# Five instruction lists made anew: block 2 and its statistics first, transposed copies ahead of evictions

## The chip, the core and the metric

The kernel runs on one core of a Trainium2 chip. The core has a matrix engine (PE, with its weight loads shown as PEld), a vector engine (DVE), an activation engine (ACT), a general engine (POOL) and a queue engine (SP) that issues most of the DMAs. The engines run side by side and wait for one another through semaphores. The metric is the device time of one execution in microseconds (us), lower is better. Before the change it is 225.8 us, the median of 3 runs from 225.59 to 225.95.

## The reference

One block of 2048 tokens of width 512 goes through a layer norm, then through two branches whose results are added to the input. All matrices are bfloat16.

```python
xn = layernorm(x)                                   # (2048, 512)
# A: 32 heads of width 16, each token sees 8 tokens back, 2 apart
q, k, v = split(xn @ wqkv)
logits[s, w] = q[s] . k[s - 2 w] / 4                # w = 0..7, masked before the start
A = (softmax(logits) weighted sum of v[s - 2 w]) @ wo
# B: gated unit with mixing over tokens
z  = gelu(xn @ w_in)                                # (2048, 1792)
z1 = z[:, :896];  z2 = layernorm(z[:, 896:])
g  = w_sp @ z2 + b_sp                               # (2048 x 2048) @ (2048 x 896)
B  = (z1 * g) @ w_out
out = x + A + B
```

## The kernel before

The tokens are cut into 16 blocks of 128 rows; x block b is loaded by the task `ldx<b>`. Each piece of work is a named task, made by a call of `T` (a compute task) or `dma` with the engine it runs on, the keys of what it reads and writes, and the function that emits its instructions. `Plan.add` derives from the keys which task has to wait for which. At the end of `build_kernel` five lists of task names (`plan.orders`: PE, ACT, DVE, POOL, SP) give the order on each engine; `Plan.schedule` follows them, and `Plan.emit` writes each engine's program in that order, with a semaphore wait wherever a task depends on another engine. An engine works strictly in its list's order: if the next task has to wait, all behind it wait too. A task of ACT's list whose name starts with `ld` or `st` issues a DMA from ACT's own queue and holds ACT's list in the same way.

The stages, in order, with the lines of the matrix work:

- Norm and transposition of blocks 0 to 3. `bnst<b>` (L665) and `bnag<b>` (L668) on DVE give mean and variance, `rstd<b>` (L670) on POOL the inverse deviation by a power, `norm<b>` (L680) on DVE the normed block. PE transposes it in two halves, `xTr<b>a` and `xTr<b>b` (L696), by a product with an identity made on POOL (`ident1`, `nident1`), and ACT copies each half out of PSUM (`xTe<b>a`, `xTe<b>b`, L703). Block 0 is transposed only centred (`ctr0`, `ctr1`, L673 and L675) for its first use; `xNr` and `xNe` (L717, L721) transpose the normed block 0 for all later uses. `warm`, `fill0` and `fill1` (L637) are products of ones that nothing reads.
- Blocks 0 to 3 times the second half of `w_in`, 448 columns at a time: `z2_<b>_<h>a` and `z2_<b>_<h>b` (L906, two products each), then `z2g<b>_<h>` on ACT (L913, gelu). The four quarters of this weight are `ldw_in2a_0`, `ldw_in2b_0` from SP and `ldw_in2a_1`, `ldw_in2b_1` from ACT; a and b are the first and second 448 columns, 0 and 1 the upper and lower rows.
- Blocks 4 to 15 are normed in the same way and transposed by a DMA from SP, `xTd<b>` (L684). For four groups of 512 tokens, `Q<j>_<c>` and `K<j>_<c>` (L749, four products each) give one quarter of the heads' queries and keys; `QKe<j>_<c>` on ACT (L757) copies the pair out, and small `halo` copies (L763) carry the last keys into the next group's buffer. `ldq` and `ldk` load the weights. `z2_4` to `z2_15` (L883) and `z2g4` to `z2g15` (L889) go on with the gated branch, `z2s<b>` (L938) sums squares on ACT.
- On DVE `prod<j>_<c>` (L772) and `padd<j>_<n>` (L780) form the logits' products; PE sums them in `lg0_0` and `lg2_0` (L807).
- `z1_<b>` (L926) and `z1g<b>` (ACT, L932) are the first half of the gate, `V<b>` (L733) and `Ve<b>` (ACT, L737) the values. `zn<b>` norms z2, partly on ACT, partly on DVE.
- The mixing over tokens in eight pairs of blocks, `P1_<t>` to `P7_<t>` (L1044), by a scheme with seven products in place of eight that needs sums made on DVE (`S13`, `S2`, `S4`, `T1` to `T4`), and the softmax (`sm`, `ssub`, `sexp`, `sz`, `srec`, `sattn`), the weighted values (`pv`, `pva`, `pvc`) and the gating (`g11` to `g22`, `u<b>`) beside it. `out<b>_0` (L1251 and L1255, eleven products) makes an output block; `fin<b>_0` copies it out and `st` stores it.

PSUM has eight banks of 512 columns, dealt out in the order in which tasks are added, so the bank of each task is the same whatever the lists say. A product may write a bank only when the copy of the bank's former content is done.

The places that matter at the start are these. x block b lies in slot b modulo 8, so `ldx8` can be issued only when all readers of block 0 (the last is `norm0`) are done. `ldx4` to `ldx7`, `ldq` and `ldk` carry a made-up read of `w_in2b_1`, which holds them on SP until that quarter has landed:

```python
for b in range(4, min(8, NB)):
    ld_x(b, "sp", after=[("w_in2b", 1)])
```

Of the kernel before, what the change touches and what calls it, by code (L numbers as in the profile page):

```python
# [14 lines left out]
class Plan:  # L15
# [313 lines left out]
def build_kernel(nc, A_x, A_wqkv, A_wo, B_x, B_w_in, B_w_sp, B_b_sp, B_w_out, out, report=False, sched_kw=None,  # L329
# [90 lines left out]
    with ExitStack() as es:  # L420
# [10 lines left out]
        def A(name, n, o2_=0):  # L431
            return ar[:, off[name] + o2_: off[name] + o2_ + n]
# [4 lines left out]
        def Fv(name, n, o2_=0):  # L437
            return fp[:, foff[name] + o2_: foff[name] + o2_ + n]
# [832 lines left out]
        for t in range(NT):  # L1271
# [11 lines left out]
            if t >= 1:  # L1283
# [3 lines left out]

        plan.orders = [
            """
                warm xTr0b fill0 xTr0a fill1 z2_0_0b z2_0_1b z2_0_0a xTr1a xTr1b z2_0_1a xNr z2_1_0a z2_1_0b z2_1_1a  # L1290
                xTr2a xTr2b z2_1_1b z2_2_0a z2_2_0b xTr3a z2_2_1a xTr3b z2_2_1b z2_3_0a z2_3_1a z2_3_1b z2_3_0b K0_3
                K0_0 K0_1 Q0_0 K0_2 Q0_1 Q0_2 Q0_3 Q1_0 K1_0 Q1_1 K1_1 K1_2 Q1_2 Q1_3 K1_3 z2_4 z2_5 z2_6 z2_7 K2_0
                Q2_0 K2_1 Q2_2 Q2_1 K2_2 Q2_3 K2_3 z2_8 z2_9 z2_10 z2_11 Q3_0 K3_0 K3_1 Q3_1 K3_2 Q3_2 K3_3 z2_12 Q3_3
                z2_13 lg0_0 z2_14 z1_14 z2_15 z1_15 z1_12 z1_13 z1_10 z1_11 z1_9 z1_8 z1_6 z1_4 z1_5 z1_7 z1_3 z1_0
                z1_2 V12 V13 V14 z1_1 lg2_0 V15 V8 V11 V10 V6 V7 V9 V4 V5 V1 V2 V0 V3 P1_0 P5_0 P6_0 P2_0 P7_0 P3_0
                P1_1 bits P4_0 P2_1 P6_1 P5_1 P7_1 P3_1 P1_2 P4_1 P5_2 P2_2 P6_2 out15_0 P7_2 P3_2 P1_3 P4_2 out14_0
                P6_3 P5_3 P2_3 P3_3 P7_3 P1_4 P5_4 out12_0 P6_4 P4_3 P2_4 out13_0 P7_4 P3_4 P1_5 P4_4 out10_0 P6_5
                P2_5 P5_5 P7_5 P3_5 out11_0 P4_5 P1_6 P5_6 out8_0 P2_6 P6_6 out9_0 P7_6 P3_6 P5_7 out6_0 P1_7 P4_6
# [5 lines left out]
                QKe1_1 halo0_2 QKe1_2 QKe1_3 z2s3 z2g4 halo0_1 z2g5 halo0_3 halo0_0 z2s4 halo1_1 halo1_0 z2g6 halo1_2
                z2g7 z2s5 QKe2_0 z2s6 QKe2_1 QKe2_2 z2s7 QKe2_3 z2g8 z2s8 z2g9 z2g10 z2s9 z2g11 z2s10 QKe3_0 z2s11
                halo2_1 QKe3_1 halo1_3 zn3 QKe3_2 zn0 z2g12 QKe3_3 halo2_2 z2g13 z2s12 lge0 z2g14 z2s13 z1g14 biasf
                z2g15 zn6 halo2_0 halo2_3 z1g15 z1g12 zn8 z1g13 z1g10 zn1 z1g11 z2s14 z1g9 z2s15 z1g8 z1g6 zn2 z1g4
                zn11 z1g5 z1g7 lge1 zn9 z1g0 z1g3 z1g2 Ve12 Ve13 zn10 zn4 Ve14 z1g1 lge2 lge3 zn5 Ve15 Ve10 zn7 Ve11
                Ve7 Ve8 Ve6 Ve4 Ve5 Ve9 ldxr0 sexp3 Ve2 cA_0 Ve3 Ve1 Ve0 cE_0 cB_0 g11_0 sexp2 cA_1 g21_0 os14_0 g11_1
                cB_1 cE_1 sexp1 os15_0 cA_2 g11_2 cB_2 ldxr1 cE_2 g21_1 ldxr2 g21_2 cA_3 cB_3 sexp0 g11_3 cE_3 os12_0  # L1310
                fin14_0 cA_4 cE_4 fin15_0 st0_0_0 cB_4 os13_0 g21_3 fin12_0 os11_0 fin13_0 g11_4 st1_0_0 ldxr3 os10_0
                ldxr4 cA_5 cB_5 cE_5 fin10_0 g21_4 g11_5 os9_0 g21_5 os8_0 cA_6 fin8_0 cB_6 fin11_0 os6_0 fin9_0
# [8 lines left out]
                bnst12 bnag14 bnag12 prod0_2 bnst15 padd0_1 norm14 bnag15 norm13 prod0_3 zv0 zq1 norm12 padd0_2 norm15
                prod1_0 zv1 prod1_2 zb0 zq2 padd1_0 zv2 padd1_1 zb1 prod2_0 zb2 prod2_2 padd2_0 zq3 prod3_2 padd2_1
                prod3_0 zv3 padd3_0 padd3_1 T3_0 zb3 T3_2 S13_0 zn13 S2_0 T1_0 zn14 zn12 smask T2_0 S4_0 zn15 T4_0
                T3_3 T3_1 T1_3 T1_1 sm1_3 sm2_3 T2_1 sm3_3 ssub3 T1_2 T2_3 T2_2 T4_3 T4_2 sz1_3 T4_1 sz2_3 sz3_3 sm1_2
                srec3 sm2_2 sattn3 sm3_2 pv14 ssub2 pv15 g22_0 sz1_2 g12_0 S13_1 sz2_2 S2_1 pva2048_0 sz3_2 sm1_1 u15
# [70 lines left out]
```

## Time and profile before

| what | value |
|---|---|
| median of 3 runs | 225.8 us (225.59 to 225.95) |
| profiled execution, whole time | 225.37 us |
| profiled execution, span from first to last instruction | 223.6 us |
| granted PE clock (mean) | 1.000 |
| PE busy | 219.7 us (98%) |
| DVE busy | 207.3 us (93%) |
| ACT busy | 134.2 us (60%) |
| POOL busy | 89.6 us (40%) |

By stage (the view that sums each engine's busy time over stretches of the span):

| stretch of the span | what runs on PE | PE | DVE | ACT |
|---|---|---|---|---|
| 0 to 5.22 us | warm-up, first transposition | 5.22 | 2.50 | 2.44 |
| 5.22 to 12.55 | blocks 0 to 3 | 7.28 | 5.34 | 5.54 |
| 12.55 to 55.40 | Q, K and z2 | 42.69 | 42.54 | 39.45 |
| 55.40 to 98.40 | logits, z1, V | 42.90 | 42.86 | 42.25 |
| 98.40 to 205.60 | mixing and outputs | 106.83 | 107.00 | 37.78 |
| 205.60 to 223.60 | the end | 15.69 | 7.08 | 6.75 |

Matmuls are pipelined and their ends are modelled, so a PE that is shown busy can hold short waits: the starts of its instructions have to be compared with the pace at which equal instructions follow each other elsewhere. In a chain of waits, a row gives start, length, engine, line and number of instructions of a piece. A row of the timeline gives start, length of one or of a merged run, engine, line, operation, shapes, and in brackets the idle time before it and what ended that.

### The profile page before, as it was taken

Reading aid. Unit: us, or ns where it says so; the run is one execution under the profiler, and the core shown is the slowest. Engines: PE = TensorE matmul, PEld = TensorE weight load, DVE = VectorE, ACT = ScalarE, POOL = GpSimd, SP = SyncE. Lnnn points to the kernel's source line nnn. Section 1 sums busy time; section 2 is a strip of 40 time slices with the busy share of each in tenths; the row PEclk is TensorE's granted clock in tenths of the full one; section 3 lists DMA queues with packets and bytes.
Section 4 is the critical chain, followed back from the end, with each engine's and each line's share of the span. In section 5 each row is a group of like instructions: output and inputs, shape, how many; then the busy total and the mean of one; then the engine's idle time right before and its main releaser. Section 6 shows DMA issues by size and latency. Waiting matters only on the chain.

```text
span 223.6 us, 3124 instructions
## 1 busy us (share of the span) xinstructions
PE 219.7 (98%) x1166; PEld 122.4 (55%) x1180; DVE 207.3 (93%) x236; ACT 134.2 (60%) x241; POOL 89.6 (40%) x38
## 2 busy tenths in 40 slices
PE   8999999999999999999999999999999999999995
PEld 7555555554677776655555454544545544444544
DVE  4699999999999999999999999999999999999810
ACT  4769899999999999977333304324304216224442
POOL 4355559965000090000000899945999900000000
DMA  6884442790000002879689997949589696428352
GB/s 222 275 185 117 97 117 51 197 201 0 3 0 0 0 0 85 176 199 215 154 166 174 233 130 157 186 118 200 173 165 228 140 193 154 99 51 179 118 104 94
DMA packets 77716, 29.96 MB, mean 134 GB/s; under 512 B 68731, under 2 KB 75401, under 8 KB 77702
## 3 DMA queue, kind: packets, MB, share of 16 engines
q1 hardware_dynamic: 74566, 25.08, 53.2%
q10 hardware_dynamic: 3136, 4.69, 6.4%
q8 instruction: 9, 0.15, 0.3%
q14 instruction: 5, 0.04, 0.1%
HBM read 9.05 MB, written 2.10 MB: 50 GB/s over the span
## 4 chain that ended last, share of the span: by engine, by line
PE 98%; issue 0%; ACT 0%
PE ps L1044 38%; PE ps L749 12%; PE ps L926 11%; PE ps L1255 11%; PE ps L883 8%; PE ps L733 6%; PE ps L1251 6%; PE ps L906 3%; PE ps L637 2%; PE ps L807 1%; PE ps L696 0%; ACT arena L703 0%; ACT arena L1264 0%; PE ps L717 0%; PE ps L1237 0%
## 5 line engine op out<-in xcount | busy, mean ns | idle before, releaser
L1044 PE MATMUL ps<-arena 128*128 128x448 f16 (+1 forms) x448 | 86.7, 352 | 0.0
L866 POOL TENSOR_TENSOR arena<-arena,fpool 128x128 bf16<-128x128 f32 x2 | 49.9, 24946 | 45.6 <-DVE arena L862 45.6
L1044 PEld LDWEIGHTS ps<-arena 128*128 128x128 f16 (+1 forms) x448 | 43.8, 98 | 41.4
L1189 DVE TENSOR_TENSOR arena<-arena 128x4096 bf16<-128x4096 bf16 x16 | 36.2, 2282 | 0.0
L772 DVE TENSOR_TENSOR arena<-arena 128x8192 bf16<-128x8192 bf16 (+1 forms) x10 | 35.5, 3555 | 0.0
L955 POOL TENSOR_TENSOR fpool<-fpool 128x4 f32<-128x4 f32 x4 | 18.1, 4541 | 27.3 <-DVE fpool L952 27.3
L749 PE MATMUL ps<-arena 128*128 128x512 bf16 x124 | 27.7, 379 | 0.2
L1193 DVE TENSOR_TENSOR arena<-arena 128x4096 bf16<-128x4096 bf16 (+1 forms) x16 | 27.9, 1745 | 0.0
L1059 ACT ACTIVATE ps<-ps 128x448 f32<-128x448 f32 x16 | 8.4, 527 | 32.4 <-PE ps L1044 24.7
L1255 PE MATMUL ps<-arena 128*128 128x512 bf16 (+2 forms) x125 | 27.1, 355 | 0.1
L780 DVE TENSOR_TENSOR arena<-arena 128x4096 bf16<-128x4096 bf16 (+1 forms) x9 | 26.9, 2992 | 0.1
L926 PE MATMUL ps<-arena 128*128 128x448 bf16 x128 | 24.7, 352 | 0.0
L670 POOL TENSOR_TENSOR fpool<-fpool 128x1 f32<-128x1 f32 x16 | 17.4, 1088 | 16.0 <-DVE fpool L668 15.7
L1062 ACT ACTIVATE arena<-ps,fpool 128x448 bf16<-128x448 f32 x16 | 10.0, 635 | 22.3 <-PE ps L1044 22.3
L926 PEld LDWEIGHTS ps<-arena 128*128 128x128 bf16 x128 | 18.5, 144 | 5.9
L749 PEld LDWEIGHTS ps<-arena 128*128 128x128 bf16 x128 | 14.5, 113 | 13.0
L1264 ACT ACTIVATE arena<-ps 128x512 bf16<-128x512 f32 (+2 forms) x17 | 9.5, 563 | 16.8 <-PE ps L1255 16.8
L883 PE MATMUL ps<-arena 128*128 128x448 bf16 x96 | 19.1, 353 | 0.0
L1255 PEld LDWEIGHTS ps<-arena 128*128 128x128 bf16 x126 | 11.9, 98 | 12.4
L757 ACT ACTIVATE arena<-ps 128x1024 bf16<-128x1024 f32 x16 | 16.1, 1028 | 2.9 <-PE ps L749 2.8
L1251 PE MATMUL ps<-arena 128*128 128x512 bf16 (+2 forms) x65 | 15.3, 353 | 0.4
L938 ACT ACTIVATE arena<-arena 128x896 bf16<-128x896 bf16 x16 | 15.3, 956 | 0.0
(86 smaller groups left out, 256.1 us busy)
## 6 DMA issues: line engine op xcount, KB each, us to landing
arena<-in_A_x_dram ACTq DMA_DIRECT2D x8, 256.0 KB, 3.6
arena<-in_A_x_dram SPq DMA_DIRECT2D x15, 128.0 KB, 3.1
out_dram<-arena ACTq DMA_DIRECT2D x7, 256.0 KB, 2.3
arena<-in_A_wqkv_dram SPq DMA_DIRECT2D x3, 512.0 KB, 4.9
arena<-in_B_w_in_dram SPq DMA_DIRECT2D x1, 896.0 KB, 5.4
arena<-in_B_w_out_dram SPq DMA_DIRECT2D x1, 896.0 KB, 6.5
arena<-arena SPq DMA_DIRECT2D x2, 448.0 KB, 4.4
arena<-arena SPq DMA_DIRECT2D x1, 672.0 KB, 5.4
```

The costliest lines, as they stand in the source:

```text
L749: last = t.matmul(bank(k + which), AC(off["wqk"] + 1024 * dc + col0, [[4, 128]]), AC(off["xnT"] + dc * S + 512 * j, [[1, 512]]), start=(dc ...
L772: T("dve", lambda v: v.tensor_tensor(pbv, qb, kb, ALU.mult), reads=[(t_, c, j) for t_ in ("QT", "KT", "KTpad") for c in cs], writes=[("pb" ...
L780: T("dve", lambda v: v.tensor_tensor(av, av, bv, ALU.add), reads=[("pb", s_) for s_ in b], writes=[("pb", s_) for s_ in a], est=c_dve(4096 ...
L866: T("pool", lambda g: g.tensor_tensor(Rv, Zv, FCa(foff["mone"], [[0, 128]]), ALU.pow), reads=[kz, "mone"], writes=[kr], est=20000, name="s ...
L883: last = t.matmul(ps[:, 512 * (k + hf): 512 * (k + hf) + HF], AC(off["xnT"] + dc * S + 128 * b, [[1, 128]]), AC(off["w_in2"] + FH * dc + H ...
L926: lastm = t.matmul(ps[:, 512 * (k + hf): 512 * (k + hf) + HF], AC(off["xnT"] + dc * S + b, [[NTOK, 128]]), AC(off["w_in1"] + FH * dc + HF ...
L955: T("pool", lambda g: g.tensor_tensor(Fv("rstd2", 4, 4 * j), Fv("msq", 4, 4 * j), mhalf, ALU.pow), reads=[("msq", j), "mhalf"], writes=[(" ...
L1044: last = t_.matmul(pb_(k_), st(k), mv(k), start=(start and k == 0), stop=(k == 7), skip_group_check=True)
L1189: T("dve", (lambda iv, tv, av: lambda v: v.tensor_tensor(tv, iv, av, ALU.mult))(iv, tv, av), reads=[("attn", q // 4)] + [("V", i_) for i_ ...
L1193: T("dve", (lambda n: lambda v: v.tensor_tensor(AC(off["Vs"], [[4096, 2], [1, n]]), AC(off["Vs"], [[4096, 2], [1, n]]), AC(off["Vs"] + n, ...
L1251: t_.matmul(po, AC(off["OT"] + 1024 * (t % 3) + 512 * r_ + 128 * cc, [[1, 128]]), AC(off["wo"] + 512 * cc + c0, [[1, n]]), start=False, st ...
L1255: last = t_.matmul(po, AC(off["z1"] + FH * tb + 128 * fc, [[1, 128]]), AC(off["w_out"] + 512 * fc + c0, [[1, n]]), start=False, stop=(fc = ...
```

## The change

All five lists are written anew; the tasks, their functions, their dependencies, buffers and banks are the same. So every engine runs the same 766 tasks in another order. What changes most at the start:

- ACT issues `ldx2` ahead of `ldw_in2b_1` in place of behind it.
- DVE runs `norm0` ahead of `bnag1`, and `bnst2`, `bnag2` ahead of `norm1`; further on `bnst8` and `bnst7` come before `norm4`, and `norm7` before `norm5` and `norm6`.
- PE runs `xNr` between `z2_0_0b` and `z2_0_1b`, both halves of `xTr1` ahead of `z2_0_0a`, and in the next stage Q tasks ahead of K tasks.
- ACT runs all eight copies `xTe0` to `xTe3` and `xNe` ahead of the eight evictions `z2g0_0` to `z2g3_1`, which it then takes in another order; the `QKe` copies of a group come in the order of the new PE list.
- POOL makes the masks `hm0` and `hm1` and the padding early and puts `nident1` behind `rstd0`.
- SP issues `ldx8` and `ldq` ahead of `ldx4` to `ldx7`, and `ldk` behind them; the transpositions come as `xTd4 xTd7 xTd5 xTd6`.

Behind the start the lists differ in the order among neighbours: for example `out14_0` comes before `out15_0`, `P4_0` before `P5_1`, `sexp0` and `sattn` tasks shift by some places, and the tail's last tasks are `out3_0 out2_0` in place of `out2_0 out3_0`. The diff, cut to the beginnings of the lists and some later lines:

```diff
-                warm xTr0b fill0 xTr0a fill1 z2_0_0b z2_0_1b z2_0_0a xTr1a xTr1b z2_0_1a xNr z2_1_0a z2_1_0b z2_1_1a
-                xTr2a xTr2b z2_1_1b z2_2_0a z2_2_0b xTr3a z2_2_1a xTr3b z2_2_1b z2_3_0a z2_3_1a z2_3_1b z2_3_0b K0_3
-                K0_0 K0_1 Q0_0 K0_2 Q0_1 Q0_2 Q0_3 Q1_0 K1_0 Q1_1 K1_1 K1_2 Q1_2 Q1_3 K1_3 z2_4 z2_5 z2_6 z2_7 K2_0
...
-                z2_13 lg0_0 z2_14 z1_14 z2_15 z1_15 z1_12 z1_13 z1_10 z1_11 z1_9 z1_8 z1_6 z1_4 z1_5 z1_7 z1_3 z1_0
...
+                warm xTr0b fill0 xTr0a fill1 z2_0_0b xNr z2_0_1b xTr1a xTr1b z2_0_0a z2_0_1a xTr2a z2_1_0a xTr2b
+                z2_1_0b z2_1_1a z2_1_1b z2_2_0a xTr3a xTr3b z2_2_1a z2_2_1b z2_2_0b z2_3_1a z2_3_0a z2_3_0b z2_3_1b
+                Q0_0 Q0_2 Q0_1 K0_1 Q0_3 K0_0 K0_3 K0_2 K1_0 K1_2 Q1_2 K1_1 Q1_1 Q1_0 z2_5 z2_4 K1_3 Q1_3 z2_7 z2_6
...
+                K3_3 z2_13 lg0_0 z2_14 z1_14 z2_15 z1_15 z1_13 z1_12 z1_10 z1_11 z1_8 z1_6 z1_9 z1_7 z1_5 z1_4 z1_0
...
-                actprime ldw_in2a_1 ldw_in2b_1 ldx2 ctr0 xTe0b xTe0a xTe1a xTe1b xNe z2g0_0 xTe2a xTe2b z2g0_1 z2g1_0
-                xTe3a xTe3b z2g2_0 z2g1_1 z2g3_0 z2g3_1 z2g2_1 QKe0_0 z2s0 QKe0_1 QKe0_2 QKe0_3 z2s1 QKe1_0 z2s2
...
+                actprime ldw_in2a_1 ldx2 ldw_in2b_1 ctr0 xTe0b xTe0a xNe xTe1a xTe1b xTe2a xTe2b xTe3a xTe3b z2g0_1
+                z2g2_1 z2g1_1 z2g2_0 z2g1_0 z2g3_1 z2g3_0 z2g0_0 QKe0_1 z2s0 QKe0_0 QKe0_3 QKe0_2 z2s1 halo0_0 z2s2
+                halo0_3 QKe1_2 QKe1_1 QKe1_0 z2s3 z2g5 halo1_0 z2g4 QKe1_3 halo0_2 z2g7 z2s4 z2g6 z2s5 QKe2_0 z2s6
...
+                z2s14 z1g15 zn5 z1g13 z1g12 z2s15 biasf z1g10 halo2_1 halo2_0 z1g11 zn3 z1g8 zn2 z1g6 z1g9 lge1 zn9
...
-                zeros steps0 steps1 bnst0 bnag0 ctr1 bnst1 bnag1 norm0 norm1 bnst2 bnag2 bnst3 norm2 bnag3 norm3 bnst4
-                bnag4 norm4 bnst5 bnag5 bnst6 norm5 bnag6 bnst7 norm6 bnag7 bnst10 bnag10 norm7 zm0_0 bnst8 zq0 bnag8
-                bnst11 prod0_0 bnag11 prod0_1 norm10 bnst9 norm8 norm11 bnag9 padd0_0 bnst13 norm9 bnst14 bnag13
...
+                zeros steps0 steps1 bnst0 bnag0 ctr1 bnst1 norm0 bnag1 bnst2 bnag2 norm1 norm2 bnst3 bnag3 norm3 bnst4
+                bnag4 bnst8 bnst7 norm4 bnag7 bnst5 norm7 bnag5 bnag8 bnst6 norm5 bnag6 bnst10 norm6 zm0_0 zq0 bnag10
+                bnst9 prod0_1 norm8 bnag9 prod0_0 bnst11 norm10 bnag11 bnst13 norm9 bnag13 padd0_0 norm11 bnst12
...
-                mhalf ident0 mone ident1 nident0 nident1 ktpad rstd0 rstd1 rstd2 rstd3 mask0 hm0 rstd4 rstd5 mask1 hm1
-                rstd6 rstd7 rstd10 rstd8 rstd11 rstd9 rstd13 rstd14 rstd12 rstd15 hm2 zr0 zr1 zr2 zr3 srec1 srec0
+                mhalf mone ident0 ktpad hm0 hm1 ident1 nident0 rstd0 nident1 rstd1 rstd2 rstd3 rstd4 rstd7 mask0 rstd5
+                mask1 rstd6 rstd8 rstd10 rstd9 rstd11 rstd13 rstd12 rstd15 hm2 rstd14 zr0 zr1 zr2 zr3 srec1 srec0
...
-                ldx0 ldx1 ldw_in2a_0 ldw_in2b_0 ldx3 ldx4 ldx5 ldx6 ldk ldx7 ldx10 ldx8 ldq ldx11 xTd4 xTd5 xTd6 xTd7
...
+                ldx0 ldx1 ldw_in2a_0 ldw_in2b_0 ldx3 ldx8 ldq ldx4 ldx5 ldx6 ldx7 ldx10 ldk ldx9 xTd4 xTd7 xTd5 xTd6
...
```

More of the change, by code (lines that the diff above doesn't have):

```diff
@@ new lines, in build_kernel @@
+                z2_1_0b z2_1_1a z2_1_1b z2_2_0a xTr3a xTr3b z2_2_1a z2_2_1b z2_2_0b z2_3_1a z2_3_0a z2_3_0b z2_3_1b
+                Q0_0 Q0_2 Q0_1 K0_1 Q0_3 K0_0 K0_3 K0_2 K1_0 K1_2 Q1_2 K1_1 Q1_1 Q1_0 z2_5 z2_4 K1_3 Q1_3 z2_7 z2_6
+                Q2_0 K2_0 Q2_2 Q2_1 K2_2 K2_1 K2_3 Q2_3 z2_9 z2_8 z2_10 K3_0 z2_11 K3_1 Q3_1 Q3_0 Q3_2 K3_2 z2_12 Q3_3
+                K3_3 z2_13 lg0_0 z2_14 z1_14 z2_15 z1_15 z1_13 z1_12 z1_10 z1_11 z1_8 z1_6 z1_9 z1_7 z1_5 z1_4 z1_0
+                z1_2 z1_3 V13 V12 z1_1 V14 lg2_0 V15 V8 V10 V11 V7 V6 V9 V4 V2 V5 V3 V0 V1 P1_0 P5_0 P6_0 P2_0 P7_0
@@ L1303, in build_kernel @@
-                xTe3a xTe3b z2g2_0 z2g1_1 z2g3_0 z2g3_1 z2g2_1 QKe0_0 z2s0 QKe0_1 QKe0_2 QKe0_3 z2s1 QKe1_0 z2s2
[L1304 to L1312, printed above, removed]
@@ new lines, in build_kernel @@
+                zn4 ldxr0 Ve9 Ve6 Ve4 Ve7 Ve5 sexp3 Ve2 Ve0 cA_0 Ve1 Ve3 cE_0 cB_0 g11_0 sexp2 cA_1 cE_1 g21_0 cB_1
+                os15_0 g11_1 os14_0 sexp1 cA_2 g11_2 cB_2 ldxr1 g21_1 cE_2 fin14_0 ldxr2 cA_3 fin15_0 g21_2 cB_3
+                os12_0 g11_3 cE_3 os13_0 sexp0 os10_0 g21_3 cA_4 fin12_0 cB_4 fin13_0 cE_4 st0_0_0 g11_4 ldxr3 os11_0
+                ldxr4 cA_5 fin10_0 g21_4 fin11_0 cB_5 cE_5 st2_0_0 os6_0 os9_0 os8_0 st1_0_0 g11_5 cA_6 g11_6 g21_5
+                cB_6 fin8_0 os7_0 fin9_0 cE_6 st3_0_0 ldxr5 cA_7 os4_0 fin6_0 ldxr6 g21_6 os5_0 ldxr7 fin5_0 cB_7 cE_7
@@ L1321, in build_kernel @@
[L1321 to L1325, printed above, removed]
@@ new lines, in build_kernel @@
+                zb0 padd0_2 zv1 prod1_0 padd1_0 zq2 padd1_1 prod2_0 zv2 prod2_2 zb1 zq3 padd2_0 prod3_2 padd2_1 zb2
+                zv3 prod3_0 padd3_0 padd3_1 T3_0 S13_0 zb3 smask T3_2 S2_0 T1_0 T1_2 S4_0 T2_2 zn12 zn13 zn15 zn14
+                T2_0 T3_3 T4_2 T3_1 T4_0 sm1_3 sm2_3 sm3_3 ssub3 T1_3 T1_1 T2_3 T2_1 T4_3 sz1_3 sz2_3 T4_1 sz3_3 sm1_2
+                srec3 sm2_2 sattn3 sm3_2 pv15 pv14 g22_0 ssub2 S13_1 g12_0 S2_1 sz1_2 pva2048_0 S4_1 sz2_2 pva1024_0
+                sz3_2 sm1_1 u14 sm2_1 pvc0 u15 sm3_1 g22_1 ssub1 S13_2 g12_1 sz1_1 S2_2 sz2_1 u12 sz3_1 sm1_0 pv12
@@ L1343, in build_kernel @@
+                w6_0 w6_1 OTd3 uT9 uT6 w7_0 w7_1 OTd4 uT7 uT5 OTd5 uT4 uT2 OTd6 uT3 OTd7 uT0 uT1 st7_1_192 st7_1_0
             """.split(),
```

38 lines of the change are left out of this document (19 added, 19 removed).

## The prediction

> **What bounds the kernel now.** I read the page first (busy shares, then the chain that ended last), then the chain in order of time, then the timeline of the start with its DMA issues, and last the stage table. The page:
>
> ```profile
> PE 219.7 (98%) x1166; PEld 122.4 (55%) x1180; DVE 207.3 (93%) x236; ACT 134.2 (60%) x241; POOL 89.6 (40%) x38
> PE 98%; issue 0%; ACT 0%
> ```
>
> PE alone carries the chain. But a busy PE can hide waits, so I compare lengths of equal pieces in the chain in order of time:
>
> ```profile
> 5.22 1.31 PE ps L906 x6
> 6.53 0.22 PE ps L696 x4
> 6.75 0.38 PE ps L906 x2
> 7.13 0.22 PE ps L717 x4
> 7.36 1.13 PE ps L906 x6
> 8.49 0.22 PE ps L696 x4
> 8.71 1.29 PE ps L906 x6
> ...
> 10.61 1.89 PE ps L906 x10
> 12.50 0.05 issue
> 12.55 10.74 PE ps L749 x49
> ...
> 60.88 21.19 PE ps L926 x112
> ```
>
> Six L906 products take 1.13 us where nothing holds them (0.189 each, as in the 10 of 1.89 and the 112 of 21.19), but 1.31 at 5.22 and 1.29 at 8.71. So PE lost 0.18 + 0.16 = 0.34 us there, and 0.25 ahead of 5.22 (first copy). From 12.55 on every piece runs at its pace: L749 at 0.216 a product, L906, L883, L926 and L1044 at 0.189, four transpositions in 0.22. The pieces of 0.05 are about as many as the matmul records that are missing (1180 loads, 1166 products), so I count them as work. A new order can't shorten that work. What it can win is below 0.34 + 0.25 = 0.6 us, all of it ahead of 12.55; what it can lose is any new wait.
>
> **The start, step by step.** The rows for it, from the timeline:
>
> ```profile
> 4.03 0.65 POOL L670 TENSOR_TENSOR fpool<-fpool 128x1 f32<-128x1 f32 x1 [1.78 <-DVE fpool L668]
> 4.18 0.69 DVE L665 BATCH_NORM_STATS2 fpool<-arena 128x6 f32<-128x512 bf16 x1
> 5.18 0.63 POOL L670 TENSOR_TENSOR fpool<-fpool 128x1 f32<-128x1 f32 x1 [0.50 <-DVE fpool L668]
> 5.22 0.87 PEld L906 LDWEIGHTS ps<-arena 128*128 128x128 bf16 x6 [0.25 <-ACT arena L703]
> 5.84 0.41 DVE L680 TENSOR_SCALAR arena<-arena,fpool 128x512 bf16<-128x512 bf16 x1 [0.46 <-POOL fpool L670]
> ```
>
> - `nident1` behind `rstd0`: rstd0 ends at 4.68, the mask takes 0.29 (L578), so the second half of block 0's transposition runs at about 5.0, not 4.69, with the three fillers (0.06 each) behind it. The first real product then starts at 5.28 instead of 5.22: +0.06.
> - `z2_0_0b` to 5.66, `xNr` (4 in 0.22) to 5.88, `z2_0_1b` to 6.26. norm0 follows bnst1 (next start 0.60 after 4.18), done by 5.2. `ldw_in2b_1` is now the third issue of ACT's queue, where x2 was; x2 was issued at 1.93 and took 3.7, and the bytes ahead of its end are the same, so the quarter lands at 5.6, ahead of 5.88. No wait.
> - `norm1` behind the statistics of block 2: bnag1 at 5.12, bnst2 at 5.23 (x2, one place earlier, is there), bnag2 at 5.95, and norm1 at 6.06, since rstd1 ends at 6.02 and bnag2 leaves DVE then: to 6.48. Before it ran 5.84 to 6.25 and PE took it up at 6.37, 0.12 later; now at 6.59. PE is free at 6.26: a wait of 0.33. Two products of block 0 are queued behind it, and so is all else.
> - From 6.59: 8 transposing products of blocks 1 (0.22), 2 and 3 (0.44), 4 products of block 0 (0.76), 24 of blocks 1 to 3 (4.54): 12.55. norm2 (7.2 for a use at 7.57), norm3 (9.1 for 9.68) and the copies, which no longer stand behind gelus on ACT, are 0.3 us or more ahead. So both waits of before are gone, and 0.06 + 0.33 come in their place: +0.39 - 0.34 = +0.05. Bounds: -0.3, if norm1 needs no wait after all; +0.3, if each copy costs its 0.05 to 0.1 of signalling again.
>
> **The loads of blocks 4 to 7.** These rows, single issues from the view of DMAs, are the last load ahead of ldk, ldk and x7, then the last transposition:
>
> ```profile
> arena<-in_A_x_dram SPq DMA_DIRECT2D x1, 128.0 KB, 3.1
> arena<-in_A_wqkv_dram SPq DMA_DIRECT2D x1, 512.0 KB, 4.9
> arena<-in_A_x_dram SPq DMA_DIRECT2D x1, 128.0 KB, 4.8
> arena<-arena SPq DMA_TRANSPOSE x1, 2.5
> ```
>
> (The first is x4, issued at 4.73.) ldx8 now holds SP until norm0 is done (5.2), then ldq until the quarter's landing (5.6); x4 to x7 follow at 6.14 to 7.55, 0.47 apart, and ldk at 8.5. ldk was issued at 6.06 and landed at 11.0, x7 at 6.54 and landed 0.34 later. With two loads fewer ahead ldq lands at 5.67 + 4.9 - 2 x 0.35 = 9.9, x4 at 10.3, x7 at 11.3. Bounds for x4: 6.14 + 3.1 = 9.2 (alone) and 6.14 + 4.9 = 11.0; I take 10.3, as x7 behind ldk is the nearest row.
> The Trainium skill, in DMA: Bandwidth & Descriptors, section "Queues, rings and completion order", says that each DMA engine takes the descriptors of one queue in ring order; x7 landing 0.34 behind ldk agrees, and this speaks against the change, since x4 now stands behind 512 KB; without the rule x4 would come at 9.3.
>
> bnst4 thus starts at 10.3 instead of 9.26. But before, DVE idled 0.67 ahead of norm3 and again ahead of norm4, and 0.1 to 0.2 three times more; now bnst8 and bnst7 fill such holes. The first product on DVE has 11 statistics and 8 norms ahead of it in both lists, and comes at 17.2 instead of 17.05. The transpositions: norm4 done at 12.75, then xTd4, xTd7, xTd5 at 1.25 each, xTd6 at 16.6 (norm6 is done at 16.3), landing 2.5 later: 19.1. K1_0 is the ninth Q or K task: 12.55 + 8 x 0.863 = 19.45. It is covered by 0.3. Price 0; if x4 comes at 11.0, 0.4. ldq (9.9 for 12.55) and ldk (13.5 for 15.1) are hidden behind PE's earlier tasks.
>
> **The rest.** PE has the same work, so I laid its list end to end at its paces, and asked of each task it needs how much work on that task's engine moved ahead of it or behind it. DVE: bnst to products -0.1 us for padd1_1 (used by lg0_0 0.9 later), 0.0 for padd3_1 (lg2_0 0.8 later), and between +5 and -5 for tasks of the mixing whose users moved too; all stay 0.5 or more ahead of PE, less the 0.15 of lateness. ACT, walked task by task with the durations of its groups: ahead of PE by 0.1 at K1_2 and z2_6, 0.35 at z2_7, 0.0 at z1_11 and z1_6, 0.2 at z1_0; elsewhere over 0.5. The same walk through the old list ends 0.1 to 0.2 later than its trace did, so the true margins are larger by that: price 0. Bound: +0.4, if the ten ACT operations ahead of z1_11 are each at the long end of their groups (zn 1.03 to 1.09, z2s 0.93 to 0.99, z1g 0.80 to 0.96). On SP, uT, OTd and w come 3 us or more ahead of their products or sums; ldxr0 on ACT waits for w_out, due at 92, ACT is there at 93.3. At the end the stores of pairs 6 and 7 go out 1 to 2 us earlier, but the last one still follows the last copy at 221.4: 0 to -0.05.
>
> **Sum.** +0.05 (start) + 0 + 0 = +0.05 on a profiled execution of 225.37 (span 223.6 and 1.8 around it). The runs' median lies 0.4 above that, so 225.8 + 0.05: 225.9 us. A difference under 0.2% (0.45 us) is about what a measurement of this kernel can't tell from none.
>
> **Rivals.**
> - Late blocks (slower): x4 to x7 land later than 10.3, xTd6 with them, and PE waits at K1_0. It decides from x4 at 10.6 on. For it: SP is held twice more, and x8 took 4.2 us from its issue once ldq was behind it. Against: ldq is hidden well, and 0.3 is free. At the bound of 11.0, with the transpositions 0.2 slower: 0.6, so 226.4.
> - ACT becomes the bound in z1 (slower): ACT is busy 42.25 of 43.0 us there, and zn5 and z2s14 now stand ahead of z1g13 and z1g12. Against: all four of the old list's tightest places (0.1 to 0.2) held. It costs up to 0.4 at z1_11 and 0.2 more at z1_6: 226.4.
> - A held power (slower): rstd takes 0.55, but 2.49 where a DVE sum runs over it (23.36), 2.92 at 33.33. rstd15 and rstd14 now fall under products; if norm14 waits for rstd14, DVE is 0.5 later, and with 0.15 and another such wait lg2_0 loses its 0.8: 226.3.
> - Faster: the start works better than I think; norm1 ahead of PE, the first copy not delayed. At most 0.6: 225.2; likelier 225.5, which is no change.
>
> **Chances.** No new wait that counts 0.50 (own range 225.5 to 226.2); late blocks 0.16; ACT 0.12; held power 0.06; a wait that I don't see, 0.5 to 2 us, 0.08; faster 0.08. Slower thus 0.42, same 0.50, faster 0.08. The range 225.3 to 226.9 leaves out part of the faster and of the unseen.
>
> **What would show it.** Right: the first L749 product at 12.5 to 12.7, a wait of about 0.3 on L680 near 6.3, bnst4 near 10.3, and no piece of the chain behind 12.55 longer than its products' pace. Wrong: a wait of PE on a DMA near 19.4, on L932 between 66 and 78, or on L780 near 86; or the first L749 product below 12.2.

## The result, and the profile after

The changed kernel takes 227.52 us (median; 226.28 to 227.92), the kernel before 225.71 us on the same chip (225.39 to 225.95): a ratio of 1.0072 with a 95% interval of 1.005 to 1.0093. I had forecast 225.9 us and a range that ended at 226.9, so the time lies outside it, on the side of the rivals that made it slower. The profiled execution shown here took 227.73 us with a span of 226.0, against 225.37 and 223.6 before. A profile is of one execution: that of the kernel before is among its shortest (it took 225.28 to 226.73 us in all that were measured), so differences between two profiles can be larger than those between medians.

The page of the changed kernel, first the busy line, then the shares of the chain that ended last:

```profile
PE 219.8 (97%) x1166; PEld 122.4 (54%) x1180; DVE 207.5 (92%) x236; ACT 134.7 (60%) x241; POOL 94.1 (42%) x38
PE 92%; DMA 3%; DVE 1%; POOL 1%; issue 1%; ACT 0%; SPq 0%; ACTq 0%
```

PE has the same work (219.7 us busy before). But the chain is no longer PE alone: 3% of it is DMA, and DVE and POOL have 1% each. The chain in order of time shows which (start, length, what):

```profile
1.42 0.49 ACTq L603
1.90 0.03 issue
1.93 5.18 DMA arena<-in_B_w_in_dram
7.11 0.05 issue
7.16 0.55 PE ps L906 x2
...
11.03 2.66 PE ps L906 x14
...
13.70 0.20 DVE fpool L668
...
16.93 0.41 DVE arena L680
...
17.72 0.58 DVE fpool L665
18.30 0.60 SPq L684
18.89 0.04 issue
18.94 2.49 DMA arena<-arena
21.43 0.14 issue
21.57 4.05 PE ps L749 x18
...
63.21 21.19 PE ps L926 x112
```

Two DMAs stand in it. The first is the quarter `ldw_in2b_1`, issued behind x2 (ACTq L603) at 1.93 and landed at 7.11. The second is the transposition `xTd6`, which ends a row of statistics and norms of blocks 4 to 7 on DVE and lands at 21.43. Behind it nothing is new: the long piece of L926 begins at 63.21, before at 60.88, 2.33 later; from there to the end the distance stays the same: the last row of the chain starts at 223.71, before at 221.38.

The timeline of the changed kernel at the places where PE, DVE and SP were held (start, length, engine, line, shapes, and in brackets the idle time before and what ended it):

```profile
5.32 0.13 PEld L696 LDWEIGHTS ps<-arena 128*128 128x128 bf16 x2 [0.49 <-issue]
5.48 0.34 SPq L603 DMA_DIRECT2D arena<-in_A_x_dram  x1
7.13 0.38 SPq L620 DMA_DIRECT2D arena<-in_A_wqkv_dram  x1
7.15 0.11 PEld L906 LDWEIGHTS ps<-arena 128*128 128x128 bf16 x2 [0.91 <-DMA arena<-in_B_w_in_dram]
7.55 0.51 SPq L603 DMA_DIRECT2D arena<-in_A_x_dram  x1
11.38 0.69 DVE L665 BATCH_NORM_STATS2 fpool<-arena 128x6 f32<-128x512 bf16 x1 [1.70 <-DMA arena<-in_A_x_dram]
21.54 0.36 PEld L749 LDWEIGHTS ps<-arena 128*128 128x128 bf16 x3 [1.44 <-issue]
```

- At 7.15 `z2_0_1b` waits 0.91 us for the quarter. The same landing frees SP: `ldx8` is out at 5.48, then SP stands until `ldq` at 7.13 (the view of SP's waits puts 1.3 us of it down to that load), and x4 follows at 7.55.
- x4 lands at 11.36, so `bnst4` begins at 11.38 behind 1.70 us of idle DVE (before at 9.26, behind 0).
- At 21.54 `K1_0` waits 1.44 us for `xTd6`.

These waits are idle times of the weight loads, and PE can lose less: before, 0.22 us of idle time at `xTr1a` delayed the products by 0.02. What PE loses is read from the starts of the products against their pace; where the two differ, both are given below.

The 2.33 us come from three places. The first L906 product starts at 5.66 instead of 5.22 (+0.44). From there to the first L749 product are 8.07 us, before 7.33 (+0.74): by the starts PE loses 0.90 at the quarter and nothing else, where before it lost 0.16 behind the copies of block 2 and 0.02 elsewhere. That puts the L749 product at 13.73 instead of 12.55 (+1.18). The rest, 1.15, is lost at `K1_0`: 31 products at 0.216 from 13.73 end at 20.42, and it starts at 21.57.

### The profile page after: what moved, and what is told of

It is laid out like the page before. It is cut to its first block, busy times and chain, and to the rows that moved or that the text cites. A ratio compares the mean times of both kernels' runs of the same rounds, so it can differ in the third digit from the quotient of the medians.

```text
span 226.0 us, 3120 instructions
## 1 busy us (share of the span) xinstructions
PE 219.8 (97%) x1166; PEld 122.4 (54%) x1180; DVE 207.5 (92%) x236; ACT 134.7 (60%) x241; POOL 94.1 (42%) x38
## 4 chain that ended last, share of the span: by engine, by line
PE 92%; DMA 3%; DVE 1%; POOL 1%; issue 1%; ACT 0%; SPq 0%; ACTq 0%
PE ps L1044 38%; PE ps L926 11%; PE ps L1255 11%; PE ps L749 9%; PE ps L883 8%; PE ps L733 6%; PE ps L1251 6%; PE ps L906 3%; DMA arena<-in_B_w_in_dram 2%; DMA arena<-arena 1%; PE ps L807 1%; POOL fpool L670 1%; DVE arena L680 1%; PE ps L696 0%; SPq L684 0%
## 5 line engine op out<-in xcount | busy, mean ns | idle before, releaser
L1044 PE MATMUL ps<-arena 128*128 128x448 f16 (+1 forms) x448 | 86.7, 352 | 0.0
L866 POOL TENSOR_TENSOR arena<-arena,fpool 128x128 bf16<-128x128 f32 x2 | 56.5, 28248 | 46.5 <-DVE arena L862 46.5
L1044 PEld LDWEIGHTS ps<-arena 128*128 128x128 f16 (+1 forms) x448 | 43.8, 98 | 41.4
L749 PE MATMUL ps<-arena 128*128 128x512 bf16 x124 | 28.2, 379 | 1.2 <-DMA arena<-arena 1.0
L926 PE MATMUL ps<-arena 128*128 128x448 bf16 x128 | 24.7, 352 | 0.0
L670 POOL TENSOR_TENSOR fpool<-fpool 128x1 f32<-128x1 f32 x16 | 16.9, 1058 | 15.3 <-DVE fpool L668 15.2
L749 PEld LDWEIGHTS ps<-arena 128*128 128x128 bf16 x128 | 14.4, 113 | 14.1 <-issue 1.4
L926 PEld LDWEIGHTS ps<-arena 128*128 128x128 bf16 x128 | 18.5, 144 | 5.9
```

Of the source, the lines that this page charges most:

```text
L670: T("pool", lambda g: g.tensor_tensor(Fv("rstd", 1, b), Fv("mv", 1, 2 * b + 1), Fv("mhalf", 1), ALU.pow), reads=[("mv", b), "mhalf"], writ ...
L749: last = t.matmul(bank(k + which), AC(off["wqk"] + 1024 * dc + col0, [[4, 128]]), AC(off["xnT"] + dc * S + 512 * j, [[1, 512]]), start=(dc ...
L866: T("pool", lambda g: g.tensor_tensor(Rv, Zv, FCa(foff["mone"], [[0, 128]]), ALU.pow), reads=[kz, "mone"], writes=[kr], est=20000, name="s ...
L926: lastm = t.matmul(ps[:, 512 * (k + hf): 512 * (k + hf) + HF], AC(off["xnT"] + dc * S + b, [[NTOK, 128]]), AC(off["w_in1"] + FH * dc + HF ...
L1044: last = t_.matmul(pb_(k_), st(k), mv(k), start=(start and k == 0), stop=(k == 7), skip_group_check=True)
```

## The experiments

L is the theory that the quarter's late landing makes both waits. S is the rival that SP's new order does it (`ldx8`, and above all the 512 KB of `ldq`, ahead of x4). D is the rival that the new order of norm1 and nident1 on DVE and POOL costs 0.3 to 0.6 us by itself. Ratios are to the kernel before, measured beside each run on the same chip, with a 95% interval. The diffs show only the stretch of a list that changes.

| run | median us | ratio |
|---|---|---|
| e1_quarter_first | 226.22 | 1.0022 (1.0006 to 1.0038) |
| e2_no_hold | 226.91 | 1.0038 (1.0017 to 1.0059) |
| e3_before_x2_first | 226.58 | 1.0024 (1.0006 to 1.0042) |
| e4_q_later | 226.14 | 1.001 (0.9992 to 1.0029) |
| g0_after_again | 227.08 | 1.0054 (1.0038 to 1.0069) |
| g1_norm1_first | 227.24 | 1.0065 (1.004 to 1.009) |
| g4_best | 226.36 | 1.0035 (1.0019 to 1.0051) |
| g5_sp_quarters_held | 229.42 (one run) | |
| g8_xTr2_later | 226.40 | 1.0034 (1.0015 to 1.0053) |
| g9_before_copies | 226.66 | 1.0029 (1.0009 to 1.0049) |
| g11_late_user | 225.82 | 0.9998 (0.9988 to 1.0008) |
| g12_late_user_nident | 225.79 | 1.0003 (0.9991 to 1.0015) |

**The quarter back in its place.** In the changed kernel, on ACT:

```diff
-actprime ldw_in2a_1 ldx2 ldw_in2b_1 ctr0
+actprime ldw_in2a_1 ldw_in2b_1 ldx2 ctr0
```

> The changed lists, with one place put back: ACT issues ldw_in2b_1 ahead of ldx2 again. Theory L (the late quarter does it all: its landing at 7.1 instead of 4.7 holds PE at z2_0_1b for 0.9 us, and holds SP's ldq and ldx4 to ldx7, so that PE waits 1.2 us again at K1_0): the quarter lands near 4.7, z2_0_1b does not wait, x4 lands near 10.4, K1_0 waits 0.3 at most; 225.9 to 226.3, a ratio of 1.001 to 1.003 to before. Rival S (SP's order, ldx8 and ldq ahead of ldx4, makes the transpositions late whatever the quarter does): K1_0 still waits 0.8 or more, 226.5 to 227. Rival D (DVE's and POOL's order, norm1 behind the statistics of block 2 and nident1 behind rstd0, costs as much): PE waits 0.3 to 0.6 ahead of xTr0a and xTr1a in place of the quarter, 226.5.

The quarter landed at 4.97, x4 at 10.45, `xTd6` at 19.36; neither `z2_0_1b` nor `K1_0` waited in this profile. But a new wait came, in the timeline of this kernel:

```profile
5.03 0.13 PEld L696 LDWEIGHTS ps<-arena 128*128 128x128 bf16 x2 [0.48 <-issue]
7.03 0.23 PEld L696 LDWEIGHTS ps<-arena 128*128 128x128 bf16 x4 [0.96 <-DVE arena L680]
```

`xTr1a` waits 0.96 us (0.69 lost) for norm1, which now stands behind the statistics of an x2 that lands at 5.74. So the first wait goes with the quarter, and the norm's new place is the next thing that is late: L is right on where the loss at the start is, D on what lies under it. That `K1_0` is free is less sure: none of the four transpositions' issues is long in this profile (1.25 to 1.31 us), while one is in 12 of the 14 profiles here. `g1_norm1_first` below, with the quarter early too and one issue of 2.03, shows a wait there again.

**The same swap in the kernel before**, and nothing else: ACT's list `actprime ldw_in2a_1 ldx2 ldw_in2b_1 ctr0`.

> The old lists, with one place of the change alone: ACT issues ldx2 ahead of ldw_in2b_1. Theory L: the quarter lands near 7.1, z2_0_1b (second product group of the old PE list) waits 1.3 us or more, x4 lands near 10.2 instead of 7.9; the old list has more room ahead of Q1_0, so little is added there: 226.8 to 227.4. Rivals S and D, in which this place does not matter much: 225.7 to 226.2.

The quarter lands at 6.73 instead of 4.71, and the timeline shows the wait at `z2_0_1b`:

```profile
6.77 0.49 PEld L906 LDWEIGHTS ps<-arena 128*128 128x128 bf16 x4 [1.32 <-DMA arena<-in_B_w_in_dram]
```

By the starts 1.05 of it is lost, and the first L749 product comes at 13.7. One swapped pair of issues thus makes the first wait in either kernel; what it costs is 0.24% (0.06 to 0.42). The time, 226.58, lies between the two forecasts.

**SP without the hold.** In the changed kernel the made-up reads of `w_in2b_1` are left out, so that `ldx8` alone holds SP:

```diff
-    512 * 512 * 2, ("wqk", which), reads=[("w_in2b", 1)],
+    512 * 512 * 2, ("wqk", which),
-ld_x(b, "sp", after=[("w_in2b", 1)])
+ld_x(b, "sp")
```

> The changed lists, without the made-up read of ldw_in2b_1 by ldq, ldk and ldx4 to ldx7, so that SP does not wait for the quarter. Theory L: z2_0_1b still waits 0.9 or more (the quarter still lands near 7.1), but ldq and x4 are issued 1.4 us earlier, x4 lands near 10, and K1_0 waits 0.3 at most: 226.3 to 226.7. Rival S: K1_0 waits 0.8 or more, 227.0 to 227.6. Rival D: no change to the 227.5 of the changed kernel at the start, and K1_0 as in S.

`ldq` goes out at 5.84 instead of 7.13, x4 lands at 10.18 instead of 11.36, and `K1_0` waits 0.2 (nothing lost), though one issue took 2.20 us. `z2_0_1b` still waits 0.92. That is L for the first wait, and for the second it says that the hold passes the quarter's lateness on. The time, 226.91, lies above L's 226.3 to 226.7 and below S's 227.0: this profile has a wait of 0.76 us at 173.31 (a weight load of L1044, behind ACT's L1246 by the view), and shorter ones of L1044 at 137.56 and 168.28, that no other profile here has; why is open.

**SP's order.** In the changed kernel:

```diff
-ldx3 ldx8 ldq ldx4 ldx5 ldx6 ldx7 ldx10 ldk ldx9
+ldx3 ldx8 ldx4 ldx7 ldx5 ldq ldx6 ldx10 ldk ldx9
```

> The changed lists, with ldq moved on SP behind ldx4, ldx7 and ldx5 instead of ahead of them. The quarter stays late in every theory, so z2_0_1b still waits 0.9 us. Theory L, as far as it goes (hold and queue together): x4 is issued at 7.1 and lands near 10.2 instead of 11.4, K1_0's wait falls from 1.2 to 0.2 or so: 226.5. If the 512 KB ahead of x4 cost nothing and the hold alone counts: x4 near 11, K1_0 waits 0.9 or more: 227.2.

With the quarter as late as ever (6.63) x4 lands at 8.64, and the timeline and the chain show one wait left:

```profile
6.67 0.11 PEld L906 LDWEIGHTS ps<-arena 128*128 128x128 bf16 x2 [0.77 <-DMA arena<-in_B_w_in_dram]
...
13.25 10.74 PE ps L749 x49
```

49 products of L749 run without a hole: `K1_0` no longer waits, with one issue of 1.76. The time is below both forecasts, and x4 came 1.6 us earlier than the 10.2 put down: 2.0 us from its issue, against 3.8 behind `ldq` in the changed kernel. So S is right that the 512 KB ahead of x4 are needed for the second wait; e2 shows that the hold on the late quarter is needed too. By medians the second wait is the larger part of the loss: 1.001 in place of 1.0054 to 1.0072. With it away the kernel can't be told from the one before (0.9992 to 1.0029).

**The changed kernel again**, with a second profile beside the next three:

> The changed kernel itself beside the others on one chip, with a second profile. Theory L with the hold: the waits at z2_0_1b (0.7 to 1.0 us) and at K1_0 are there again, x4 lands at 10 to 11.5; the part of K1_0's wait that came with the issue of one transposition taking 2.43 us instead of 1.25 may be missing or on another transposition, so K1_0 waits 0.3 to 1.5 us and the time is 226.5 to 227.7. If the wait at K1_0 were a matter of chance alone, it would be gone and the time 226.2 or less.

Both waits are there again, and the time is in the first range: 0.96 at `z2_0_1b` (the quarter at 6.79) and 1.46 at `K1_0` (1.17 lost); x4 lands at 11.04. One issue is long here too (1.97 us, `xTd4`). The first L906 product comes at 5.28, so most of the +0.44 of the first profile belongs to that execution.

**Norm1 first**, on top of the quarter in its old place:

```diff
-actprime ldw_in2a_1 ldx2 ldw_in2b_1 ctr0
+actprime ldw_in2a_1 ldw_in2b_1 ldx2 ctr0
-bnst1 norm0 bnag1 bnst2 bnag2 norm1 norm2
+bnst1 norm0 bnag1 norm1 bnst2 bnag2 norm2
```

> The changed kernel with two undos at its start: the quarter second on ACT's queue, and norm1 ahead of the statistics of block 2 again; SP's list, the hold and nident1 stay as changed. Theory D (each order at the start only uncovers the next wait: with the quarter early, norm1 behind bnag2 costs 0.8 us): the wait ahead of xTr1a falls from the 0.96 that the quarter-first kernel showed to about 0.3, the first L749 product comes at about 12.3 instead of 12.8; K1_0, which had 0.3 to spare there, then waits 0 to 0.4 us for xTd6, so the time is 225.7 to 226.0. Against it (the 0.96 is the landing of x2, not the order on DVE): the wait stays above 0.8, the time stays at 226.2.

A miss. The wait at `xTr1a` fell to 0.13, as D said, but `xTr2a`, which the changed list of PE draws ahead of three tasks of block 1, now found norm2 late, by 1.06 us (0.78 lost), and the first L749 product stayed at 13.5. `K1_0` waited 0.43 (0.14 lost), behind the long issue of 2.03. The profiled execution, 226.49, was the shortest of only four; what the others, up to 227.82, waited for isn't known.

**All early undos at once**: the two above, nident1 ahead of rstd0, `xTr1a xTr1b` behind `z2_0_0a`, and on SP:

```diff
-ldx3 ldx8 ldq ldx4 ldx5 ldx6 ldx7 ldx10 ldk ldx9
+ldx3 ldx4 ldx8 ldx7 ldx5 ldq ldx6 ldx10 ldk ldx9
```

> The changed kernel with every early undo at once: quarter second on ACT's queue, norm1 ahead of bnst2, nident1 ahead of rstd0, xTr1a and xTr1b behind z2_0_0a, and on SP x4, x7, x5 ahead of ldq; its lists for the later stages stay as changed. If all the loss lies ahead of K1_0, this one has none of it: first L749 product at 12.1 to 12.4, x4 landing at about 8.5, no wait at K1_0, and a time within 0.2 of the kernel before: 225.5 to 225.9. If the changed lists of the later stages cost something of their own, K1_0 is reached as before and the time is still 226.2 or more.

Also a miss, at the same place (1.10 lost); the timeline:

```profile
8.37 0.11 PEld L696 LDWEIGHTS ps<-arena 128*128 128x128 bf16 x2 [1.37 <-DVE arena L680]
```

This is `xTr2a` again. The changed lists of the later stages, which I had named as the other explanation, are not the cause: the piece of 112 L926 products begins 48.4 us behind the first L749 product here (61.91 and 13.53, with a wait of 0.27 at `K1_0` in it), 48.3 before (60.88 and 12.55).

**And block 2's transposition back behind block 1's products:**

```diff
-z2_0_1a xTr2a z2_1_0a xTr2b z2_1_0b z2_1_1a z2_1_1b z2_2_0a xTr3a
+z2_0_1a z2_1_0a z2_1_0b z2_1_1a xTr2a xTr2b z2_1_1b z2_2_0a xTr3a
```

> The kernel with all early undos of the fourth-from-last study run (quarter second, norm1 ahead of bnst2, nident1 ahead of rstd0, xTr1 behind z2_0_0a, ldq behind x4, x7, x5), and besides it the transpositions of block 2 put back behind the products of block 1 on PE, as before. There PE waited 0.9 to 1.0 us at xTr2a for norm2, because that transposition had been drawn ahead of three tasks of block 1. If the orders of the start are one set (norm2 comes at 8.2 once norm1 is first, so xTr2a must be late too), this wait falls to 0.3 or less and the first L749 product comes at 12.2 to 12.5. K1_0 then is due at about 19.3 and xTd6 lands at 18.8 if no transposition's issue is long, at 20.1 if one is: 225.6 to 226.4, most likely 226.0. If the start stays at 13.0 or later, something else of the changed start holds it.

The wait at `xTr2a` is nearly gone (0.19), but 0.42 each at `z2_1_0a` and `z2_2_0a` for copies (0.15 lost each) and 0.95 at `xTr3a` for norm3 (0.68 lost) have come, and the first L749 product stays at 13.5. Undoing the start piece by piece moved the wait from one block to the next. PE's new list takes the transpositions of blocks 1 and 2 one to three tasks earlier; that DVE's row of norms would have to be as early for all of them is an explanation that no run tested.

**The copies alone, in the kernel before:**

```diff
-z2_0_0b z2_0_1b z2_0_0a xTr1a xTr1b z2_0_1a xNr z2_1_0a
+z2_0_0b xNr z2_0_1b z2_0_0a xTr1a xTr1b z2_0_1a z2_1_0a
-xTe0b xTe0a xTe1a xTe1b xNe z2g0_0 xTe2a xTe2b z2g0_1
+xTe0b xTe0a xNe xTe1a xTe1b xTe2a xTe2b z2g0_0 z2g0_1
```

> The kernel before with one part of the change alone: xNr ahead of z2_0_1b on PE, and on ACT the copies xNe, xTe2a, xTe2b ahead of the gelu of block 0. It fills the wait of 0.22 at xTr1a and the 0.16 behind the copies of block 2. If PE's early waits were each a loss of their own, 0.3 us go: 225.4. If the row of norms sets the pace (norm2 ends at 8.16 whatever PE does), the gain at xTr1a comes back as a longer wait at xTr2a, and 0 to 0.15 is left: 225.5 to 225.7, no difference that can be told.

Neither number was right: it is slower. Three gelus (`z2g0_0`, `z2g0_1`, `z2g1_0`) now stand together ahead of the copies of block 3, where two did; PE waits for copies (L703) three times, last and longest at 12.24 (0.15, 0.15 and 0.55 lost), where the kernel before lost 0.16 once:

```profile
8.04 0.11 PEld L906 LDWEIGHTS ps<-arena 128*128 128x128 bf16 x2 [0.42 <-ACT arena L703]
...
9.94 0.11 PEld L906 LDWEIGHTS ps<-arena 128*128 128x128 bf16 x2 [0.42 <-ACT arena L703]
...
12.24 0.11 PEld L906 LDWEIGHTS ps<-arena 128*128 128x128 bf16 x2 [0.83 <-ACT arena L703]
```

And there was less to win than I put down: the wait of 0.22 at `xTr1a` in the kernel before was the weight load's and cost PE 0.02. About 0.5 us more of this profile is PE's slow start (below), which is no part of the edit.

**What makes the third place late.** In the changed kernel SP's quarters, and all behind them, wait for ACT's last one; ACT's queue is untouched. In the loop that makes the loads of the quarters h = 0 is SP's (the edit also adds ACT's last quarter first, so that the others can depend on it):

```diff
-                    256 * n * 2, (nm, h), writes=[(nm, h)], name="ld%s_%d" % (nm, h))
+                    256 * n * 2, (nm, h), reads=[("w_in2b", 1)] * (1 - h), writes=[(nm, h)], name="ld%s_%d" % (nm, h))
```

> The changed kernel with SP's two quarters of w_in2 (and all that stands behind them on SP) held until ACT's last quarter has landed; ACT's queue is untouched, with that quarter third and the same 576 KB on it. Theory Q (the two queues share the DMA engines, so what stands ahead of the third place is ACT's own 576 KB and about as much of SP's): with only x0 and x1 (256 KB) on SP's queue the quarter lands at 4.6 to 5.2 instead of 6.6 to 7.1. Rival (the third place on ACT's own queue, or its later issue at 1.93, makes it late): it still lands at 6.3 or later. The time says nothing here: the held quarters are themselves late, 2 us or more are lost at the start.

The quarter's row in the view of DMAs (KB, us from issue to landing), here:

```profile
arena<-in_B_w_in_dram ACTq DMA_DIRECT2D x1, 224.0 KB, 3.7
```

and in the changed kernel:

```profile
arena<-in_B_w_in_dram ACTq DMA_DIRECT2D x1, 224.0 KB, 5.2
```

It lands at 5.63: between the two expectations. SP's quarters take 0.6 to 1.5 us of it (6.21 to 7.11 in the seven profiles where it is third and SP is free to issue); the rest, 0.9 above the 4.71 of before, can be its place and its later issue. That part isn't shown: this is one execution, and as second load the quarter landed anywhere from 4.71 to 5.72 in six profiles.

**The user moved instead of the load.** On PE, and SP's order as in e4_q_later:

```diff
-z2_0_0b xNr z2_0_1b xTr1a xTr1b z2_0_0a z2_0_1a
+z2_0_0b xNr z2_0_0a xTr1a xTr1b z2_0_1b z2_0_1a
```

> The changed kernel with x4, x7, x5 ahead of ldq on SP, and on PE the one user of the late quarter moved behind what does not need it: z2_0_0b, xNr, z2_0_0a, xTr1a, xTr1b, and then z2_0_1b. The quarter still comes third on ACT's queue and lands at 6.6 to 7.1. Theory L (the loss at the start is only the place where PE meets that landing): PE works 0.6 us more ahead of z2_0_1b, its wait falls from 0.77 to 0.2 or less, the first L749 product comes at 12.3 to 12.6 instead of 12.84, K1_0 does not wait, and the time is 225.6 to 225.9, no difference from the kernel before that can be told. If the row of norms holds the start as well (norm2 and norm3 no earlier than 7.2 and 9.3), the gain comes back as waits at xTr2a or xTr3a and the time stays at 226.1.

225.82 us: by the median the loss is gone. The profile, of this kernel's slowest execution (226.22), misses the other half of the forecast: the first L749 product comes at 13.33, not at 12.3 to 12.6. The quarter lands at 7.01 and costs 0.20, as forecast, but PE now meets other loads. `z2_0_0a`, now the second z2 task, waits 0.42 for SP's `ldw_in2a_0`, which landed at 6.20 (5.07 to 5.93 in the other profiles where SP's quarters aren't held); and the first L749 products wait 0.55 for `ldq` (0.31 lost), which landed at 13.04 now that it stands behind x4, x7 and x5. `K1_0` doesn't wait. The second kernel has nident1 ahead of rstd0 besides:

> The same with nident1 ahead of rstd0 on POOL, as before. If nident1's place behind rstd0 costs PE its 0.30 to 0.49 at xTr0a, the first product comes 0.2 to 0.3 earlier and so does the end: 225.4 to 225.6. If it only trades (rstd0, norm0 and norm1 come 0.3 later then, and PE meets that at xTr1a), the time is that of the kernel without it, within 0.2.

225.79, the same: that place only trades. This profile is of its shortest execution (225.40); its page's chain, and the chain in order of time:

```profile
PE 98%; issue 0%; ACT 0%
...
12.58 10.74 PE ps L749 x49
```

PE carries the chain alone again, and the first L749 product stands where it stood before (12.55). One issue of a transposition takes 2.27 us here, and `K1_0` doesn't wait. Two edits, `ldq` behind x4, x7 and x5 and `z2_0_1b` behind `xTr1b`, take the whole loss back by the median. The first alone already leaves none that can be told, so what the second adds is seen in profiles only. Nothing here beats the kernel before.

## Why the prediction was wrong

The likeliest case, no new wait that counts, failed; of the rivals, the late blocks came true, and larger, beside a wait at the start that no rival had.

1. **The quarter: "the bytes ahead of its end are the same, so the quarter lands at 5.6".** This is the step that failed first. I took the landing of x2 in the third place (5.64) for that of the quarter. It landed at 7.11, and at 6.2 to 7.1 in the seven profiles with it third, where x2 as third lands at 5.64 to 6.16 in six. The landing was a term with no bounds, and the wait behind it, 0.77 to 1.32 where PE's list left `z2_0_1b` early, was not among the rivals. e1 and e3 show that the swap makes it, in both kernels.
2. **nident1 at +0.06, norm1 with a wait of 0.33, and the old waits at 0.34.** The wait at `xTr0a` was 0.49, but x0 landed 0.27 later in that profile than before; in the second profile (g0) the first L906 product comes at 5.28, the number put down, and moving nident1 back gains nothing that can be told (225.79 and 225.82). Norm1's wait did not show in the changed kernel, since the quarter's was longer and covers it; with the quarter early it is 0.96, because x2 is late then (e1). And 0.16 of the old 0.34 was never lost: the chain's 1.31 for six products at 5.22 runs to the modelled end of the last one, while by the starts (5.22, then L696 at 6.37; rows at the end of this document) they took 1.15. Rightly read, the sum of the start would have been +0.39 - 0.18 = +0.21 instead of +0.05; the profile has +1.18.
3. **x4 at 10.3, with bounds of 9.2 and 11.0.** It landed at 11.36. The working behind it held: x4 came 0.35 behind `ldq`, as put down, and 4.2 us after `ldq`'s issue (10.3 - 5.67 = 4.6 put down). But that issue hangs on the quarter, 7.13 instead of 5.67, so the first error passes through the hold into the second estimate. My bounds let the queue vary and took the quarter for certain.
4. **The transpositions "at 1.25 each, xTd6 at 16.6", and `K1_0` "covered by 0.3. Price 0".** `norm4` and the first transposition follow `bnst4` as put down (xTd4 2.43 behind it). One of the four issues took 2.43 us, not 1.25; the view of line L684, first the changed kernel, then the kernel before:

```profile
L684 SPq DMA_TRANSPOSE arena<-arena x4: 1264/1284/2427, 13.8 to 18.9; - x4
...
who waited for it (us, times):
  PEld ps L749: 1.4, 1
  PE ps L749: 1.0, 1
```

```profile
L684 SPq DMA_TRANSPOSE arena<-arena x4: 1200/1260/1312, 11.3 to 15.8; - x4
```

   So `xTd6` landed at 21.43, 2.3 later than I put it: 1.1 from x4 and 1.2 from that issue. `K1_0` was due at 20.42, 1.0 later than the 19.45 put down, and started 0.14 behind the landing, at 21.57: 1.15 lost. Either term alone would have left little of it; in g0 the long issue (1.97) is about 0.7 of the 1.17. The pace of 1.25 was read from the one profile of before; of the 14 profiles only that and e1's have no long issue. So how much of the second wait comes with x4 and how much with the long issue changes from one execution to the next, and no run held the long issue fixed. The rival "late blocks" had the mechanism and its place right; its threshold (10.6) wasn't tested, and its 226.4 was too small, as it put 0.2 on slower transpositions.
5. **The rest, price 0.** Right: DVE, ACT and SP behind `K1_0` add nothing, and the rivals on ACT in z1 and on a held power did not come about.
6. **The signs.** "no piece of the chain behind 12.55 longer than its products' pace" was the right thing to watch, and "a wait of PE on a DMA near 19.4" was on the list of what would show me wrong; it came at 21.5. The quarter's wait was not on it.

By medians the second wait is the larger loss: with it away 226.14 are left (1.001), with the first away as well 225.82 (0.9998), though these two intervals overlap. With the quarter early and all else as changed (e1) 226.22 are left, the norm's wait.

## What to carry to other kernels

A load that moves back one place in a queue can't be priced by the landing of another load in that place: here the two differ by 0.8 us, and what the other queue has in flight makes 0.6 to 1.5 us. Where a hold or a wait on it stands in an issuing engine's list, every estimate behind it needs that landing's bounds, not its middle. Compare lengths by the starts of instructions: a chain's row that runs to a modelled end showed a wait here that wasn't there. When an order made anew loses, undoing its parts one at a time can only uncover the next wait: moving the one user that meets the late load (225.82, with `ldq` moved too) came out better here than moving the load back (226.22).

## What the runs showed of the hardware

**Two queues share the engines.** With SP's quarters held, ACT's third load took 3.7 us in one execution, instead of 4.3 to 5.2 in seven. The Trainium skill, DMA: Bandwidth & Descriptors, section "Issuing engines are not separate DMA queues", says that DMAs started by different engines interleave on the same 16 DMA engines; that agrees. Why x2 and the quarter land 0.8 us apart in the same place (means of 5.9 and 6.8), though either ends the same 576 KB of ACT's queue, stays open; they differ in size (128 and 224 KB).

**A transposition's issue can double.** Each of the four at the start held SP for 1.20 to 1.31 us in the profiles of the kernel before and of e1, but one of the four took 1.75 to 2.43 in the other twelve. In the packets of the trace a fetch of 16 KB on the instruction queue starts at 12.9 and 12.75 in those two, and at 13.9 to 16.7 in the twelve, where it overlaps the long issue. But in those two it overlaps an issue of normal length. That the fetch causes it wasn't tested.

**PE's pace at the start varies.** The timeline of g9_before_copies, and then of the kernel before, at the first products of L906:

```profile
5.42 0.95 PE L906 MATMUL ps<-arena 128*128 128x448 bf16 x2
...
6.54 0.73 PE L906 MATMUL ps<-arena 128*128 128x448 bf16 x3
```

```profile
5.22 1.31 PE L906 MATMUL ps<-arena 128*128 128x448 bf16 x6
6.37 0.39 PE L696 MATMUL ps<-arena 128*128 128x128 bf16 x4
```

Two products take 0.95 in the first, 0.37 from one start to the next, where the pace is 0.19 (six from 5.22 to 6.37 in the second). By the starts of equal products PE comes to full pace at about 4.1 us in the changed kernel's profile, at about 4.5 in that of before, and at 6.4 in this one, though the granted clock reads 1.00 throughout. The Trainium skill, TensorE: Matmul & The Clock Gate, Part 1, has PE at half its clock until a free-running window of 3.4 us has seen it busy; first products at 0.84 and a full pace that comes at another time in each profile agree with that; the shortest delay here, 2.7 us (full pace at 3.5 in g5_sp_quarters_held), is below that window and doesn't fit it. It cost about 0.5 us in this one execution (two products of L906 and four of L717 at half pace: 2 x 0.18 and 4 x 0.05) and can be part of why executions of one kernel differ by over 1 us; that was not tried.
